# Sliding-window attention feeding a multiplicative FFN: batch 1's transposes moved into the weight fold, two products per unit in batch 1, the range check on Pool and a hinted branch

## Chip, cores, metric

One core of a Trainium2 chip runs the whole kernel. The metric is the device time of one execution in microseconds (us); a run's figure is the time of the slowest core, and here there is one.

## What is computed

Attention over a window of 64 keys (8 batches, 8 heads, 576 tokens, head size 64), then a feed-forward layer whose two branches are multiplied, on 4608 tokens of width 512:

```python
scores = scale * np.matmul(q, k.transpose(0, 1, 3, 2))
mask = (rel >= 0) & (rel < window)            # rel = query - key, window = 64
scores = np.where(mask, scores, -1000000000.0)
scores = scores - np.max(scores, axis=-1, keepdims=True)
attn = np.exp(scores)
attn = attn / (np.sum(attn, axis=-1, keepdims=True) + 1e-09)
x = np.matmul(attn, v)                        # heads side by side: [4608, 512]
a = x @ w1                                    # [512, 1024]
b = x @ w2
out = (a * b @ w3) @ w_out                    # w3 [1024, 1024], w_out [1024, 512]
```

## The kernel before

The code runs under a manual schedule: what is written first is issued first on its engine, so the order of the Python statements is the order of the work on PE, DVE, ACT, Pool and SP. Nothing is reordered by a scheduler.

**Attention.** A batch is six units, numbered `d` (batch 0 has 0 to 5, batch 1 has 6 to 11, batch 2 begins at 12). A unit is two pairs of heads on 192 queries. `scores(d)` (line 267) makes 4 matmuls into PSUM tile `s_ps`, an Exp on ACT (L282) into `pt`, and band masks by pairs of affine selects on Pool (L291, L293): four selects for the first two units of a batch, two for the others. `values(d)` (line 297) makes 8 matmuls (L312) into `o_ps` that carry the row sums beside the values, two Ln and one Exp on ACT (L321 to L324) and two multiplies on DVE (L327, L328) into `xT`. No maximum is subtracted; the logarithms of the sums are kept (`keep_sums`, L333, DMAs from SP's queue into `lnsum`), and at the end `check_sums` tests that they lie in bounds and counts those that don't. After all stores, `tc.If(bad > 0)` (L644) runs a general path if the count isn't zero.

**Transposes.** Q and K come as f32 (`load_qk`), are cast to f16 (`cast_qk` in two halves, L216; `cast_third` for batch 0, L223), and are transposed by PE in three groups of six blocks (`transposes`, L254). A group goes into PSUM tile `tp`, of which there is one, or into one half of a `spare` tile, made from the two banks of `s_ps` or `o_ps`. DVE evacuates K (L258); each Q group is evacuated by ACT for the one half of the partitions and DVE for the other (both L263).

**Fold.** At the start w3 and w_out are folded into one matrix `wc`, in 8 steps: `fold_t` transposes a piece of w3 (8 transposes L447, evacuated by DVE at L449 into `t2k`), `fold_mm` multiplies it (8 matmuls L455, cast into `wc_sb` at L456). One fold step stands behind each unit of batch 0.

**Products.** Each group of 512 tokens needs 8 `ffn_ab` (8 matmuls of 512 columns, L396; ACT copies `a` at L401, DVE multiplies by `b` at L402) and 4 `ffn_o` (8 matmuls L409; copy by DVE at L411, store by SP at L418). There are 9 groups, so 108 products of 8 matmuls. Group 0's are written out by hand among the units of batch 1. From batch 2 on a table `slots` gives each product a due unit, and `tick(u)` issues the attention up to it, with the transposes, casts and loads of later batches from the table `late`.

**Fillers.** `keep_busy(n)` (line 473) makes n small matmuls on the identity into `tp` that compute nothing needed. `ones_of(i)` (L489) writes the ones beside V, once for each of two V buffers, on Pool.

**End of the program.** After `tick` has issued the last attention unit, 12 products are left; `check_sums` is issued after the 4th of those counted by `quiet` (line 633), on DVE and one PE matmul (L470).

Of the kernel before, what the change touches and what calls it, by code (L numbers as in the profile page):

```python
# [15 lines left out]
P = 128  # L16
# [128 lines left out]
def kernel(  # L145
# [100 lines left out]
    def transposes(b, which, c, tp=None, late=True):  # L246

        if c == 0 and which == "k":
            kTs[b] = sb.tile([P, NJ, S], FP16, name="kT")
        t16 = (k16s if which == "k" else q16s)[b]  # L250
        if tp is None:
            tp = ps_t.tile([P, 6, P], FP16, name="tp")
        for i in range(6):
            nc.tensor.transpose(tp[:, i, :], t16[:, 6 * c + i, :], ident16)  # L254
        src = tp.rearrange("q i (p j) -> q j p i", p=TP)
        if which == "k":
            cp = dve_cp if late or c != 1 else act_cp
            cp(kTs[b].rearrange("q j (p i) -> q j p i", i=TI)[:, :, :, 6 * c:6 * c + 6], src)  # L258
        else:
            qT = qTs[b % 2]  # L260
            for lo, a, cp in ((0, 0, act_cp), (D, 1, dve_cp)):
                dst = qT[lo:lo + D, :, a, :].rearrange("q j (p i) -> q j p i", i=TI)
                cp(dst[:, :, :, 6 * c:6 * c + 6], src[lo:lo + D])  # L263
# [193 lines left out]

    def check_sums():

        rows = 2 * 3 * B  # L460
# [3 lines left out]
        okv = const.tile([rows, 1], FP32)  # L464
        nc.vector.tensor_reduce(okv, chk, axis=mybir.AxisListType.X, op=ALU.min)
        nc.vector.tensor_scalar(okv, okv, -1.0, 1.0, op0=ALU.mult, op1=ALU.add)
        ones = const.tile([rows, 1], FP32)
        nc.vector.memset(ones, 1.0)
        c_ps = ps_t.tile([1, 1], FP32, name="tp")
        nc.tensor.matmul(c_ps, okv, ones, start=True, stop=True)  # L470
        nc.vector.tensor_copy(bad_i[0:1, :], c_ps)
# [19 lines left out]
    ones_of(0)  # L491
    load_wo()
# [4 lines left out]
    ones_of(1)  # L497
# [9 lines left out]
    def spare(pool, name):  # L507

        t = pool.tile([P, 2, 512], FP32, name=name).bitcast(FP16)
        return [t[:, i, 0:768].rearrange("p (i n) -> p i n", i=6) for i in range(2)]  # L510
# [23 lines left out]
    for d in range(6):  # L534
# [6 lines left out]
        if d == 0:  # L541
            load_v(1, 0, 2)
        if d == 1:
            load_v(1, 3)
            load_qk(1, "k", nc.vector.memset)
            load_qk(1, "q")
# [16 lines left out]
    transposes(1, "k", 1)  # L563
    ffn_ab(0, 0)
    transposes(1, "k", 2)
    ffn_ab(0, 1)
    tps = spare(ps_v, "o_ps")
    for c in range(3):
        transposes(1, "q", c, tps[c] if c < 2 else None)
    ffn_ab(0, 2)  # L570
    load_v(1, 5)
    scores(6)
    copy_v(1, 1)
    ffn_ab(0, 3)
    scores(7)
    for d in range(6, 12):
        values(d)
        if d < 10:
            scores(d + 2)
            ffn_ab(0, d - 2)  # L580
        else:
            ffn_o(0, d - 10)
            store()
        if d == 7:
            copy_v(1, 4)
            load_qk(2, "k", nc.gpsimd.memset)
            load_qk(2, "q")
            load_v(2, 0, 2, 3)
        if d == 9:
            load_v(2, 4, 5)  # L590
    cast_qk(2, "k", 0, pool_cp)
    cast_qk(2, "k", 1, pool_cp)
    transposes(2, "k", 0)
    ffn_o(0, 2)
    store()
    transposes(2, "k", 1)
    ffn_o(0, 3)
    store()
    transposes(2, "k", 2)
    cast_qk(2, "q", 0, pool_cp)  # L600
    cast_qk(2, "q", 1, pool_cp)
    load_qk(3, "k")
# [7 lines left out]
    for g in range(1, NG):  # L610
# [8 lines left out]
    todo = {0: [lambda: transposes(2, "q", 0), lambda: copy_v(2, 1)],  # L619
            1: [lambda: transposes(2, "q", 1), lambda: copy_v(2, 4), lambda: cast_qk(3, "k", 0, pool_cp)],  # L620
            2: [lambda: transposes(2, "q", 2), lambda: cast_qk(3, "k", 1, pool_cp)]}
    u = 24
    quiet = 0
    for i, (w, due) in enumerate(slots):
        store()
        w()
        for fn in todo.get(i, []):
            fn()
# [10 lines left out]
    assert u == NU + LAG + 5 and quiet >= 4  # L639
# [4 lines left out]
    with tc.If(bad > 0, preferred_fallthrough_block=False):  # L644
# [30 lines left out]
```

## Time and profile before

| what | value |
|---|---|
| time, median of 3 runs | 317.93 us (316.24 to 318.02) |
| time of the profiled execution | 317.97 us |
| span of the profile (first to last instruction) | 316.2 us |
| PE busy | 280.5 us, 89% |
| DVE, ACT, POOL busy | 201.9, 176.8, 179.1 us |
| chain that ended last, by engine | PE 73%, DVE 9%, ACT 7%, issue 4%, POOL 4% |

The span begins at 0 with the first instruction. The profiled execution lasted 1.8 us longer than its span. The page gives busy time by engine and by group of instructions; a timeline lists instructions in order of their start, with the idle time of the engine just before them in brackets and the instruction that ended it; the view of stretches gives for each stretch the busy time of every engine and, as PEclk, the granted clock of PE (1.00 is full, 0.50 is half).

### The profile page before, as it was taken

What the parts mean: (1) busy time and instruction counts of PE and PEld (TensorE: products, weight loads), DVE (VectorE), ACT (ScalarE), POOL (GpSimd) and SP (SyncE); (2) the same over time, 40 slices, a digit from 0 to 9 for tenths busy, and PEclk for the clock granted to TensorE, in tenths of its full rate; (3) what the DMA queues carried; (4) which work ended last, traced back from release to release, by engine and by line L of the source; (5) the groups of instructions that cost most, each with busy time, mean ns of one, the idle gap of its engine ahead of it and who ended that gap; (6) DMA issues with size and microseconds to landing.
All of it is one profiled execution on the core that took longest, in us unless ns stands there. A gap on an engine that the chain in (4) does not pass through costs nothing.

```text
span 316.2 us, 5497 instructions
## 1 busy us (share of the span) xinstructions
PE 280.5 (89%) x2027; PEld 165.4 (52%) x2027; DVE 201.9 (64%) x307; ACT 176.8 (56%) x294; POOL 179.1 (57%) x211
## 2 busy tenths in 40 slices
PE   8578959677897999999999999999999999996880
PEld 8465524344354465655555797555555555542330
DVE  6646586645577478678777866598678655445340
ACT  2333723577334677786777665587588756522200
POOL 9664980079906896789669554885694452200000
PEclk9869997999999799999999999999999999999796
DMA  7999997006969294766729370940190030030021
GB/s 256 215 180 198 207 286 77 0 1 122 267 234 391 97 84 136 293 43 103 261 106 91 131 290 2 158 55 1 66 143 2 2 134 2 0 135 0 4 102 41
DMA packets 51668, 38.87 MB, mean 123 GB/s; under 512 B 38784, under 2 KB 41856, under 8 KB 51632
## 3 DMA queue, kind: packets, MB, share of 16 engines
q0 software_dynamic: 41744, 9.96, 34.5%
q1 hardware_dynamic: 9888, 28.46, 24.9%
q8 instruction: 18, 0.29, 0.4%
q14 instruction: 18, 0.15, 0.2%
HBM read 38.80 MB, written 9.44 MB: 153 GB/s over the span
## 4 chain that ended last, share of the span: by engine, by line
PE 73%; DVE 9%; ACT 7%; issue 4%; POOL 4%; DVEq 0%; POOLq 0%; ACTq 0%
PE f_ps L396 33%; PE f_ps L409 18%; PE o_ps L312 6%; PE s_ps L277 5%; PE tp L254 4%; PE tp L477 3%; DVE qT L263 2%; PE f_ps L455 2%; POOL pt L291 2%; ACT ln_s L322 2%; ACT qT L263 2%; ACT r L324 2%; DVE xT L328 1%; POOL pt L293 1%; ACT pt L282 1%
## 5 line engine op out<-in xcount | busy, mean ns | idle before, releaser
L396 PE MATMUL f_ps<-xT,w_sb 128*128 128x512 f16 (+1 forms) x640 | 137.5, 364 | 0.7 <-DVE ab L402 0.7
L291 POOL TENSOR_SCALAR_AFFINE_SELECT pt<-pt 128x512 f16<-128x512 f16 (+1 forms) x64 | 52.8, 825 | 74.6 <-ACT pt L282 74.6
L396 PEld LDWEIGHTS <-w_sb 128*128 128x128 f16 x640 | 60.9, 99 | 52.2 <-issue 4.6
L409 PE MATMUL f_ps<-wc_sb,ab 128*128 128x512 f16 x288 | 67.1, 379 | 0.1
L402 DVE TENSOR_TENSOR ab<-f_ps,a_sb 128x512 f16<-128x512 f32 x72 | 49.7, 691 | 24.1 <-PE f_ps L396 20.1
L401 ACT COPY a_sb<-f_ps 128x512 f32<-128x512 f32 x72 | 41.7, 579 | 33.3 <-PE f_ps L396 32.7
L282 ACT ACTIVATE pt<-s_ps 128x1024 f16<-128x1024 f32 (+1 forms) x48 | 45.6, 950 | 24.9 <-PE s_ps L277 22.4
L327 DVE TENSOR_TENSOR xT<-o_ps,r 64x384 f16<-64x384 f32 x48 | 26.4, 549 | 48.3 <-ACT r L324 45.9
L293 POOL TENSOR_SCALAR_AFFINE_SELECT pt<-pt 128x512 f16<-128x512 f16 (+1 forms) x64 | 52.8, 825 | 4.4
L321 ACT ACTIVATE ln_s<-o_ps 64x384 f32<-64x384 f32 x48 | 23.4, 487 | 45.8 <-PE o_ps L312 45.8
L409 PEld LDWEIGHTS <-ab 128*128 128x128 f16 x288 | 27.0, 98 | 27.6 <-issue 0.3
L235 POOL DMA_DIRECT2D v<-in_v_dram x40 | 34.7, 873 | 4.7 <-DMA ab<-in_moe_w_out_dram 2.9
L312 PE MATMUL o_ps<-pt,v 128*128 128x128 f16 (+1 forms) x384 | 28.0, 215 | 8.2 <-DVE xT L328 4.3
L312 PEld LDWEIGHTS <-v 128*128 128x128 f16 x384 | 23.6, 98 | 20.8 <-issue 6.6
L411 DVE COPY t2k<-f_ps 128x512 f32<-128x512 f32 x36 | 24.9, 692 | 9.5 <-PE f_ps L409 8.8
L277 PE MATMUL s_ps<-qT,kT 128*128 128x256 f16 x192 | 27.9, 269 | 1.5 <-DVE qT L263 0.9
L328 DVE TENSOR_TENSOR xT<-o_ps,r 64x384 f16<-64x384 f32 x48 | 26.9, 561 | 0.6
L324 ACT ACTIVATE r<-ln_s 128x384 f32<-128x384 f32 x48 | 25.1, 523 | 1.5
L277 PEld LDWEIGHTS <-kT 128*128 128x128 f16 x192 | 18.1, 100 | 11.4 <-issue 2.7
L263 DVE COPY qT<-tp 64x768 f16<-64x768 f16 x20 | 19.2, 960 | 7.6 <-ACT qT L263 7.3
L322 ACT ACTIVATE ln_s<-o_ps 64x384 f32<-64x384 f32 x48 | 23.1, 482 | 0.6
L258 DVE COPY kT<-tp 128x768 f16<-128x768 f16 x21 | 20.0, 951 | 1.8 <-PE tp L254 1.6
(61 smaller groups left out, 200.2 us busy)
## 6 DMA issues: line engine op xcount, KB each, us to landing
stage<-in_k_dram SPq DMA_DIRECT2D x16, 576.0 KB
stage<-in_q_dram SPq DMA_DIRECT2D x16, 576.0 KB
out_dram<-t2k SPq DMA_DIRECT2D x36, 256.0 KB
v<-in_v_dram POOLq DMA_DIRECT2D x32, 128.0 KB, 5.1
w_sb<-in_moe_w_dram POOLq DMA_DIRECT2D x4, 512.0 KB, 9.1
ab<-in_moe_w_out_dram POOLq DMA_DIRECT2D x1, 1024.0 KB, 11.9
ab<-in_moe_w_dram POOLq DMA_DIRECT2D x2, 512.0 KB, 14.3
xT<-in_moe_w_dram POOLq DMA_DIRECT2D x2, 512.0 KB, 18.1
```

The lines of the kernel that those rows point to most:

```text
L235: nc.gpsimd.dma_start(out=vh[lo:P, c], in_=v[b, :, s0:s0 + P - lo, :].rearrange("h s d -> s h d"))
L263: cp(dst[:, :, :, 6 * c:6 * c + 6], src[lo:lo + D])
L277: nc.tensor.matmul(s_ps[:, jj, c0:c0 + 2 * n].rearrange("k (a n) -> k a n", a=2), kT[:, 2 * jp + jj, k0:k0 + P], qT[:, 2 * jp + jj, :, q0: ...
L282: nc.scalar.activation(pt[:, :, 0:w], s_ps[:, :, 0:w], AF.Exp, bias=-SHIFT, scale=scale)
L291: nc.gpsimd.affine_select(out=sl, in_=sl, pattern=pat, compare_op=ALU.is_ge, fill=0.0, base=off, channel_multiplier=-1)
L293: nc.gpsimd.affine_select(out=sl, in_=sl, pattern=[[-s, m] for s, m in pat], compare_op=ALU.is_ge, fill=0.0, base=63 - off, channel_multip ...
L312: nc.tensor.matmul(o_ps[:, jj, o0:o0 + n], v16[:, si * 2 + bi, j0 + jj, a * D:a * D + P], pt[:, jj, c0 + a * n:c0 + a * n + n], start=firs ...
L324: nc.scalar.activation(r, y, AF.Exp, scale=-1.0)
L396: nc.tensor.matmul(d[:, f * n + c0:f * n + c1], w[:, dc, (fc + f) * P:(fc + f + 1) * P], xT[:, dc, xc:xc + c1 - c0], start=first, stop=(dc ...
L401: act_cp(a_sb[:, 0:nf * n], a_ps[:, 0:nf * n])
L402: nc.vector.tensor_tensor(ab[:, fc:fc + nf, lo:hi], b_ps[:, 0:nf * n].rearrange("p (f n) -> p f n", f=nf), a_sb[:, 0:nf * n].rearrange("p ...
L409: nc.tensor.matmul(o_ps, ab[:, fc, t * P:t * P + P], wc_sb[:, fc, :], start=(fc == 0), stop=(fc == 7))
```

## The change

**Start.** The second `ones_of` is issued ahead of the weight loads on Pool instead of behind them. The evacuation of batch 0's three Q groups is written so that ACT and DVE take turns on the tiles (q0 on ACT with q1 on DVE, q2 on ACT with q0 on DVE, q1 on ACT with q2 on DVE), where before ACT and DVE took the same tile one after the other. `keep_busy` before `scores(0)` has 15 matmuls for 10, and there is one more of 10 before the fold. `transposes` returns the evacuating function if asked (`evac=False`), and `spare` makes its tile as f16 `[P, 2, 1024]`.

**End of the fold.** Batch 1's K casts stand behind unit 3, one unit earlier. Its K and Q transposes stand around unit 5 and the last fold step, all through `s_ps` spares and `tp`; before, they were spread over the first three products of group 0.

**Batch 1.** Units 6 to 9 have two products each, 10 one, and none stands between `scores(7)` and `values(6)`. Batch 2's Q and K are loaded at the end of the fold, and cast by Pool at units 7 to 10. Its transposes stand around unit 11 with three products left beside them; before, seven products stood between them, and the Q groups ran beside group 1's first three (table `todo`, which is gone).

**First units of batch 2.** The due times of group 1 rise by a quarter of the lead with each of its first four products (`ahead`); before, the first three were due at once.

**Check and branch.** The square and the comparison move from DVE to Pool and are issued after the 2nd of the last products; the count (`count_bad`: one PE matmul and a cast on DVE) after the 6th. The If is laid out with its true block as the fall-through, so that the compare itself jumps past the general path; a branch hint is named at the place of the count.

The diff, cut to its core:

```diff
@@ transposes @@
-            for lo, a, cp in ((0, 0, act_cp), (D, 1, dve_cp)):
-                dst = qT[lo:lo + D, :, a, :].rearrange("q j (p i) -> q j p i", i=TI)
-                cp(dst[:, :, :, 6 * c:6 * c + 6], src[lo:lo + D])
+        def half(a, cp):
+            dst = qT[a * D:a * D + D, :, a, :].rearrange("q j (p i) -> q j p i", i=TI)
+            cp(dst[:, :, :, 6 * c:6 * c + 6], src[a * D:a * D + D])
+        if not evac:
+            return half
+        half(0, act_cp)
+        half(1, dve_cp)
@@ check_sums @@
-        nc.vector.tensor_tensor(chk, lnsum, lnsum, ALU.mult)
-        nc.vector.tensor_single_scalar(chk, chk, BOUND * BOUND, op=ALU.is_le)
+        nc.gpsimd.memset(ones, 1.0)
+        nc.gpsimd.tensor_tensor(chk, lnsum, lnsum, ALU.mult)
+        nc.gpsimd.tensor_single_scalar(chk, chk, BOUND * BOUND, op=ALU.is_le)
         nc.vector.tensor_reduce(okv, chk, axis=mybir.AxisListType.X, op=ALU.min)
         nc.vector.tensor_scalar(okv, okv, -1.0, 1.0, op0=ALU.mult, op1=ALU.add)
-        nc.vector.memset(ones, 1.0)
+    def count_bad():
@@ start @@
     ones_of(0)
+    ones_of(1)
     load_wo()
...
-    ones_of(1)
     load_v(0, 4, 5)
...
-    transposes(0, "q", 0, tps[3])
-    transposes(0, "q", 1)
-    transposes(0, "q", 2, spare(ps_s, "s_ps")[0])
-    keep_busy(10)
+    q0 = transposes(0, "q", 0, tps[3], evac=False)
+    q1 = transposes(0, "q", 1, evac=False)
+    q2 = transposes(0, "q", 2, spare(ps_s, "s_ps")[0], evac=False)
+    q0(0, act_cp)
+    q1(1, dve_cp)
+    q2(0, act_cp)
+    q0(1, dve_cp)
+    q1(0, act_cp)
+    q2(1, dve_cp)
+    keep_busy(15)
     scores(0)
     keep_busy(10)
     scores(1)
+    keep_busy(10)
@@ fold @@
-    for d in range(6):
+    for d in range(5):
...
         if d == 0:
             load_v(1, 0, 2)
+            load_qk(1, "k", nc.vector.memset)
+            load_qk(1, "q")
...
         if d == 3:
             load_v(1, 4)
-        if d == 4:
             cast_qk(1, "k", 0, dve_cp)
             cast_qk(1, "k", 1, dve_cp)
-            cast_qk(1, "q", 0, pool_cp)
-            transposes(1, "k", 0)
+    cast_qk(1, "q", 0, pool_cp)
     cast_qk(1, "q", 1, dve_cp)
+    tps = spare(ps_s, "s_ps")
+    transposes(1, "k", 0, tps[0])
+    transposes(1, "k", 1, tps[1])
+    values(5)
+    transposes(1, "k", 2)
+    fold_step(7)
...
+    tps = spare(ps_s, "s_ps")
+    transposes(1, "q", 0, tps[0])
+    transposes(1, "q", 1, tps[1])
+    transposes(1, "q", 2)
@@ batch 1 @@
+    steps = [lambda fc=fc: ffn_ab(0, fc) for fc in range(2, 8)] + [lambda t=t: ffn_o(0, t) for t in range(3)]
+    for d in range(6, 11):
         values(d)
         if d < 10:
             scores(d + 2)
-            ffn_ab(0, d - 2)
+        for _ in range(2 if d < 10 else 1):
+            steps.pop(0)()
+            store()
...
+    tps = spare(ps_s, "s_ps")
+    transposes(2, "k", 0, tps[0])
+    transposes(2, "k", 1, tps[1])
+    values(11)
+    transposes(2, "k", 2)
...
     ffn_o(0, 3)
...
+    transposes(2, "q", 0, tps[0])
+    transposes(2, "q", 1, tps[1])
+    transposes(2, "q", 2)
@@ slots @@
-        first = 3 if g == 1 else 0
-            share = max(0, i + 1 - first) / (len(part) - first)
-            slots.append((w, lo + (hi - lo) * share + (LAG + 1) * (i >= first)))
+            ahead = (LAG + 1) * (min(1, (i + 1) / 4) if g == 1 else 1)
+            slots.append((w, lo + (hi - lo) * (i + 1) / len(part) + ahead))
@@ end @@
-            if quiet == 4:
+            if quiet == 2:
                 check_sums()
+            if quiet == 6:
+                count_bad()
+                tc.mark_branch_hint_location("range", "LikelyTaken", mybir.ALL_ENGINES)
...
-    with tc.If(bad > 0, preferred_fallthrough_block=False):
+    with tc.If(bad > 0, preferred_fallthrough_block=True, label="range"):
```

In the changed kernel the lines stand 4 to 20 further down: the select pairs are L297 and L299, values L318, products L402 and L415, their evacuations L408 and L417, the fold L453 to L462, the If L664.

Three places show how the order moves. The first is Pool at the start, where `v_0_85` and `v_1_86` are the two V buffers with their ones, and the DMAs behind them fetch w_out, pieces of w3 and blocks of V. Before:

```order
L489 MEMSET v_0_85 128x48x64
L434 DMA ab<-in_moe_w_out_dram 128x8x512
L440 DMA ab<-in_moe_w_dram 128x2x1024
L235 DMA v_0_85<-in_v_dram 128x8x64 x3
L440 DMA ab<-in_moe_w_dram 128x2x1024
L440 DMA xT<-in_moe_w_dram 128x2x1024 x2
L489 MEMSET v_1_86 128x48x64
```

Of the change:

```order
L498 MEMSET v_0_85 128x48x64
L498 MEMSET v_1_86 128x48x64
L440 DMA ab<-in_moe_w_out_dram 128x8x512
L446 DMA ab<-in_moe_w_dram 128x2x1024
L235 DMA v_0_85<-in_v_dram 128x8x64 x3
L446 DMA ab<-in_moe_w_dram 128x2x1024
L446 DMA xT<-in_moe_w_dram 128x2x1024 x2
```

The second memset now stands ahead of all weight loads.

The second place is DVE at the end of the fold, from the cast of `wc` of fold step 5 to the last evacuation of batch 1's Q. Before:

```order
L456 CAST wc_sb<-f_ps 128x512
L216 CAST k_597<-stage 128x18x64 x2
L258 COPY kT<-tp 128x128x6
L327 TENSOR_TENSOR xT<-o_ps,r 64x2x192
L328 TENSOR_TENSOR xT<-o_ps,r 64x2x192
L216 CAST q_600<-stage 128x18x64
L258 COPY kT<-tp 128x128x6
L402 TENSOR_TENSOR ab<-f_ps,a_sb 128x512
L258 COPY kT<-tp 128x128x6
L402 TENSOR_TENSOR ab<-f_ps,a_sb 128x512
L263 COPY qT_88<-o_ps 64x4x32x6 x2
L263 COPY qT_88<-tp 64x4x32x6
```

Of the change:

```order
L216 CAST k_578<-stage 128x18x64 x2
L333 TENSOR_TENSOR xT<-o_ps,r 64x2x192
L334 TENSOR_TENSOR xT<-o_ps,r 64x2x192
L455 COPY t2k<-f_ps 128x1024
L462 CAST wc_sb<-f_ps 128x512
L216 CAST q_618<-stage 128x18x64
L258 COPY kT<-s_ps 128x128x6 x2
L333 TENSOR_TENSOR xT<-o_ps,r 64x2x192
L334 TENSOR_TENSOR xT<-o_ps,r 64x2x192
L258 COPY kT<-tp 128x128x6
L264 COPY qT_88<-s_ps 64x4x32x6 x2
L264 COPY qT_88<-tp 64x4x32x6
```

The products' multiplies (L402) no longer stand between the evacuations, and the K casts stand one fold step earlier. The first group of a spare tile is evacuated before the second group's transposes into the other half are let go, in both kernels.

The third place is DVE at the check. Before, behind the fifth product from the last attention unit:

```order
L402 TENSOR_TENSOR ab<-f_ps,a_sb 128x512 x5
L462 TENSOR_TENSOR chk<-lnsum 48x768
L463 TENSOR_SCALAR chk<-chk 48x768
L465 TENSOR_REDUCE okv<-chk 48x1
L466 TENSOR_SCALAR okv<-okv 48x1
L468 MEMSET ones 48x1
L471 CAST bad_i<-tp 1x1
L402 TENSOR_TENSOR ab<-f_ps,a_sb 128x512 x3
```

Of the change:

```order
L408 TENSOR_TENSOR ab<-f_ps,a_sb 128x512 x3
L474 TENSOR_REDUCE okv<-chk 48x1
L475 TENSOR_SCALAR okv<-okv 48x1
L408 TENSOR_TENSOR ab<-f_ps,a_sb 128x512 x4
L480 CAST bad_i<-tp 1x1
L408 TENSOR_TENSOR ab<-f_ps,a_sb 128x512
L417 COPY t2k<-f_ps 128x512 x4
```

The reduce stands two products earlier, and four products stand between it and the cast of the count. On every engine's list a row BRANCH_PREFETCH_HINT stands at the very start of the program, behind the first jump, and the unconditional jump behind the compare is gone.

More of the change, by code (lines that the diff above doesn't have):

```diff
@@ L244, with transposes @@
     kTs = {}
-    def transposes(b, which, c, tp=None, late=True):
+    def transposes(b, which, c, tp=None, late=True, evac=True):
         if c == 0 and which == "k":
@@ L507, in spare @@
     def spare(pool, name):
[L509 removed]
+        t = pool.tile([P, 2, 1024], FP16, name=name)
         return [t[:, i, 0:768].rearrange("p (i n) -> p i n", i=6) for i in range(2)]
@@ L579 @@
             scores(d + 2)
-            ffn_ab(0, d - 2)
-        else:
[L582 to L596, printed above, removed]
+        for _ in range(2 if d < 10 else 1):
+            steps.pop(0)()
+            store()
+        if d == 6:
+            load_v(2, 4, 5)
+            copy_v(1, 4)
+            load_qk(3, "k")
+        else:
+            which, hh = [("k", 0), ("k", 1), ("q", 0), ("q", 1)][d - 7]
+            cast_qk(2, which, hh, pool_cp)
+    tps = spare(ps_s, "s_ps")
[3 more added lines that the diff above has]
+    transposes(2, "k", 2)
+    for hh in range(2):
+        cast_qk(3, "k", hh, pool_cp)
     ffn_o(0, 3)
     store()
[L599 to L602, printed above, removed]
+    tps = spare(ps_s, "s_ps")
+    transposes(2, "q", 0, tps[0])
+    transposes(2, "q", 1, tps[1])
+    transposes(2, "q", 2)
+    copy_v(2, 1)
+    copy_v(2, 4)
     load_qk(3, "q")
@@ L638 @@
     store()
-    assert u == NU + LAG + 5 and quiet >= 4
+    assert u == NU + LAG + 5 and quiet >= 6
     fast.close()
```

34 lines of the change are left out of this document (11 added, 23 removed).

## Prediction

> **What bounds the kernel now.** I read the page's sums first, then the view of stretches, cut where the program's stages meet: start, fold to unit 2, end of the fold with batch 1's transposes, batch 1 with batch 2's transposes, first units of batch 2, steady state.
>
> ```profile
> span 316.2 us, 5497 instructions
> ...
> 0.00:20.50 20.50, 14.07 (x149) 13.35 (x150) 12.53 (x13) 6.67 (x8) 14.72 (x19) 0.84 1.19 219
> 20.50:37.30 16.80, 14.74 (x127) 8.86 (x126) 9.40 (x18) 8.61 (x14) 12.07 (x17) 0.99 1.31 184
> 37.30:61.20 23.90, 17.37 (x128) 9.58 (x129) 16.79 (x25) 9.93 (x17) 9.17 (x10) 0.93 0.74 153
> 61.20:98.50 37.30, 31.27 (x213) 16.54 (x213) 22.85 (x38) 21.48 (x36) 24.04 (x28) 1.00 0.77 171
> 98.50:110.50 12.00, 10.23 (x71) 5.63 (x71) 6.03 (x8) 6.81 (x12) 9.01 (x13) 0.86 0.51 202
> 110.50:281.20 170.70, 169.92 (x1247) 101.77 (x1246) 122.67 (x189) 118.59 (x200) 110.05 (x127) 1.00 0.51 100
> ```
>
> After the bounds and the length come PE, PEld, DVE, ACT and POOL busy, then the granted clock. From 110.5 on PE works 169.92 of 170.70 us: nothing but less PE work would help there, and the change takes none away. Idle PE lies ahead of that (6.4 us at the start, 2.1, 6.5, 6.0, 1.8) and behind it. A product costs 8 x 0.216 = 1.73 us at full clock (row L396 of the check's fence: 24 matmuls at full clock would be 5.2). The change can save only idle time and half-clock time in these stages.
>
> The clock follows idleness. These stretches are 3.3 to 3.5 us long:
>
> ```profile
> 44.60:48.10 3.50, 0.87 (x15) 0.87 (x16) 2.87 (x5) 0.00 (x0) 2.02 (x2) 0.99 1.26 207
> 48.10:51.50 3.40, 3.40 (x12) 1.16 (x10) 2.30 (x4) 1.49 (x3) 0.00 (x0) 0.50 1.37 137
> 55.00:58.30 3.30, 1.41 (x17) 0.94 (x16) 1.98 (x3) 1.29 (x2) 0.00 (x0) 1.00 0.00 0
> 99.30:102.70 3.40, 1.63 (x20) 1.19 (x19) 1.91 (x2) 1.40 (x2) 2.60 (x5) 1.00 1.02 412
> 102.70:106.10 3.40, 3.40 (x10) 1.31 (x9) 1.15 (x3) 2.08 (x4) 3.27 (x5) 0.50 0.58 236
> ```
>
> PE 0.87 busy of 3.50 was followed by 3.4 us at half clock, and so was 1.63 of 3.40; 1.41 of 3.30 was not. A half-clock stretch costs 1.7 us where PE is the bound.
>
> **Check (E).** The first of the two holes behind 281.2:
>
> ```profile
> 282.54 0.48 SPq L333 DMA_DIRECT2D lnsum<-ln_s  x1
> ...
> 286.65 0.69 DVE L402 TENSOR_TENSOR ab<-f_ps,a_sb 128x512 f16<-128x512 f32 x1 [1.04 <-PE f_ps L396]
> ...
> 293.46 0.19 PE L470 MATMUL tp<-ones,okv 48*1 48x1 f32 x2 [3.46 <-DVE ones L468]
> 293.58 7.04 PE L396 MATMUL f_ps<-xT,w_sb 128*128 128x512 f16 x24
> ```
>
> PE stood 3.46 us for the count's matmul, and then 24 product matmuls took 7.04 us, 1.8 more than at full clock. With four products between the reduce and the count, both go, and the count's own 0.1 stays: 3.46 + 1.84 - 0.1 = **-5.2**. The cover: the last sums are issued at 282.54, and the DMA view of 282 to 286 us, in slices of 0.1, ends with this traffic:
>
> ```profile
> GB/s 410 348 103 0 0 0 0 0 0 143 348 369 471 369 389 328 267 0 0 0 0 0 82 0 0 0 0 0 0 0 0 0 0 0 0 0 0 0 0 0
> ```
>
> The last of it lies in the 23rd slice, so they have landed by 284.3. The reduce stands on DVE behind the third product's multiply, done at 286.65 + 0.69 = 287.3. So Pool has 3.0 us for two operations of 768 columns (the memset of 48 x 1 beside them waits for nothing) that this trace does not have on Pool. Nearest rows:
>
> ```profile
> L291 POOL TENSOR_SCALAR_AFFINE_SELECT pt<-pt 128x1024 f16<-128x1024 f16 x32 | 36.0, 1124 | 38.3 <-ACT pt L282 38.3
> ...
> L489 POOL MEMSET v<- 128x3072 f16 x2 | 5.4, 2684 | 0.0
> ```
>
> At 0.87 to 1.10 ns a column, 768 take 0.7 to 0.85 us each, 1.7 for both. Two f32 inputs may cost several times that; at 3 us each the reduce, and with it DVE's next product multiply, would come 2.9 us late, so the gain's bounds are -5.4 and -2.3. I take -5.2, since the rows lie near.
>
> **Branch (F).** From the lists by source line, with durations in ns (min/median/max) and first and last start:
>
> ```profile
> L644 PEldq COMPARE_BRANCH  x2: 95/1872/3650, 304.2 to 307.7; - x2
> L644 DVEq COMPARE_BRANCH  x2: 51/53/55, 308.2 to 308.4; - x2
> L644 SPq COMPARE_BRANCH  x2: 38/46/53, 309.3 to 311.8; - x2
> ```
>
> ```profile
> L670 SPq EVENT_SEMAPHORE  x14: 17/28/28, 314.6 to 316.2; - x14
> ...
> L670 DVEq DRAIN  x2: 10/34/59, 311.8 to 315.7; - x2
> ```
>
> SP compares at 309.3, falls through, waits for the stores until 311.8, jumps past the general path, and shows its next instruction at 314.6: 2.75 us for a jump. DVE's took 3.4. After the change the compare at 309.3 is the jump, beside the landing of the stores. Without help from the hint SP arrives at 309.3 + 2.75 to 3.4 = 312.05 to 312.7 instead of 314.6, so -2.55 to -1.9; with the target fetched ahead the stores set the end, -2.8. If a second jump stays behind the first, its 3.4 eats all this and 0.7 more. I take **-2.2**, without help: the hint is issued 300 us ahead of the branch.
>
> **Start (A).**
>
> ```profile
> L223 DVE CAST k<-stage x2: 560/741/922, 6.6 to 7.0; 128x768 f16<-128x768 f32 x2
> L223 DVE CAST q<-stage x2: 541/1300/2060, 11.6 to 13.6; 128x768 f16<-128x768 f32 x2
> ```
>
> ```profile
> 13.72 0.67 PE L254 MATMUL o_ps<-ident,q 128*128 128x128 f16 x6 [2.47 <-DVE q L223]
> ...
> 15.26 0.96 DVE L263 COPY qT<-o_ps 64x768 f16<-64x768 f16 x1 [1.13 <-ACT qT L263]
> ...
> 17.15 1.23 PE L477 MATMUL tp<-ident 128*128 128x128 f16 x10 [1.48 <-DVE qT L263]
> ...
> 20.52 1.18 PE L447 MATMUL f_ps<-ident,ab 128*128 128x128 f16 x16
> ```
>
> DVE's first q cast took 2.06 us where others take 0.55, beside Pool's 2.7 us memset. With the memset earlier the cast ends 1.5 sooner. DVE's evacuations now start on q1 while ACT has q0, instead of 1.13 late, three of 0.96 in a row: from about 13.0 to 16.0, where before the third ended at 17.01 + 0.96 = 17.97. That is -2.0, and ten more fillers ahead of the fold give back 0.7 to 1.2: **-1.3**. Pool's memset now delays the issue of the weights by 2.7 us. I estimate that this costs nothing, since K and Q hold the DMA engines for the first 8 us anyway; at worst all 2.74 arrive at the fold, which then starts 0.9 late. Bounds -1.7 and +0.9.
>
> **End of the fold (B).** Before, 37.3 to 61.2 us, with three products in it. Its DVE rows, and the wait in its middle:
>
> ```profile
> 41.25 0.68 DVE L456 CAST wc_sb<-f_ps 128x512 f16<-128x512 f32 x1
> ...
> 45.37 1.80 DVE L216 CAST k<-stage 128x1152 f16<-128x1152 f32 x2
> 47.23 0.51 PE L254 MATMUL tp<-ident,k 128*128 128x128 f16 x6 [3.77 <-DVE k L216]
> ...
> 47.78 0.96 DVE L258 COPY kT<-tp 128x768 f16<-128x768 f16 x1 [0.60 <-PE tp L254]
> ...
> 49.79 0.55 DVE L327 TENSOR_TENSOR xT<-o_ps,r 64x384 f16<-64x384 f32 x1 [1.06 <-ACT r L324]
> ```
>
> After the change DVE is a chain from fold step 5's cast on, which ends 4.65 us into the stage: K casts 1.80 (6.45), two multiplies 1.15 (7.6), w3 copy and wc cast 1.4 (9.0), Q cast 0.76 (9.75), first kT 0.96 (10.7). Only then may the second K group use the tile's other half (0.5), and values(5) stands behind it on PE (0.6), its Ln, Ln, Exp take 1.6 (13.35), multiplies 1.15 (14.5), third kT 0.96, first Q half 0.96 (16.4), second Q group 0.5, ACT's half 0.81, DVE's two 1.92: 19.7. One product is inside; the other two cost 3.46 later: 19.7 + 3.5 - 23.9 = -0.7. To that I add 1.2: PE waits from about 6.95 to 10.7 as it did for 3.77 before, so the clock falls again, this time with the transposes and values(5) on the chain. And 0.4, since the K casts fall beside Pool's selects, as the two took 1.80 beside a Pool DMA issue instead of 1.5; 0 to 1.2. Together **+0.9** (-1.5 to +2).
>
> [...]
>
> **Batch 1 (C).**
>
> ```profile
> 71.63 0.61 PE L312 MATMUL o_ps<-pt,v 128*128 128x128 f16 x8 [0.71 <-DVE xT L328]
> ...
> 75.11 0.61 PE L312 MATMUL o_ps<-pt,v 128*128 128x128 f16 x8 [0.71 <-DVE xT L328]
> ```
>
> A unit takes 3.48 us, of which PE waits 0.71 for the multiplies of the unit before. With two products a unit PE has 0.44 + 0.45 + 2 x 1.73 = 4.4 and waits for nothing. So 3.7 to values(6), as now, four units of 4.4, then the same serial chain as in B without casts: multiplies end 3.15 after values(10) starts, t2k 0.69 and kT 0.96 (4.8), second K group and values(11) 0.95, Ln to multiplies 2.65 (8.4), kT 0.96, t2k 0.69, Q 0.96 (11.0), group 0.4, ACT 0.81, DVE 1.92: 14.1. Sum 35.4 with 12 products, before 37.3 with 13: -0.2. Two gaps of PE of about 2.5 and 3 us are new there, with one product between them; by the stretch 99.3 to 102.7 the clock falls: +0.9, since half of what runs then waits anyway. **+0.7** (-1.5 to +2.5).
>
> [...]
>
> **First units of batch 2 (D).**
>
> ```profile
> 99.94 0.49 PE L277 MATMUL s_ps<-qT,kT 128*128 128x256 f16 x4 [0.62 <-ACT pt L282]
> ...
> 102.22 0.45 PE L312 MATMUL o_ps<-pt,v 128*128 128x64 f16 x7 [0.65 <-POOL pt L293]
> ...
> 108.42 0.50 PE L312 MATMUL o_ps<-pt,v 128*128 128x128 f16 x8
> ```
>
> From scores(12), at 98.5, to values(13), at 108.42, 9.9 us hold two products, waits on Exp and selects, and 1.7 of half clock. After the change a product stands between the two scores and another ahead of values(12): three products, three scores, one values and three transposes are 5.2 + 1.35 + 0.45 + 1.2 = 8.2 without a wait. 8.2 - 1.73 - 9.9 = **-3.5** (-4 to -1, if the clock falls here anyway).
>
> **Sum.** -1.3 + 0.9 + 0.7 - 3.5 - 5.2 - 2.2 = -10.6, to the profiled execution's 317.97 (the span 316.2 and 1.8 around it; the median of the runs shown is 317.93): **307.4 us**.
>
> **The rivals.** (1) The clock holds in the transposes' gaps and casts and selects miss each other: B and C lose their 1.2, 0.4 and 0.9, 304.9 us. For it: 55.0 to 58.3. Against: the other two stretches. (2) The front end nets nothing: the serial chains behind half tiles give back what A and D bring; E and F alone make 310.6. For it: the chain's many evacuations, each of which adds its semaphore hops, and DVE has 16.8 of 23.9 us busy in B already. Against: D's waits are plainly gone. (3) The check or the branch brings little: Pool slow, 310.3, or no gain from the jump, 309.6. For it: no Pool arithmetic on two f32 inputs in the trace; against: 3.0 us of cover. (4) Slower: the hint, at the program's start, turns each engine's instruction fetch away from its sequential path, and later fetches are not ahead of the engine. The place is PE, the price that of its 3.65 us behind the branch for each lost fetch; the third makes up the gain, from the fourth it is slower, five give 307.4 + 18.3 = 325.7. For it: only that price; against: nothing says that a hint acts before its branch. (5) Rivals (2) and (3) together: a check that keeps only its 2.3 and nothing else, 315.7. That the change doesn't do what it says: a hint too early is that for the branch, and is already left out of F.
>
> **Numbers.** Forecast 0.37, (1) 0.2, (2) 0.18, (3) 0.13, (4) 0.05, (5) 0.07. A measurement of this kernel tells about 1%, 3.2 us, from no change. All of the first four are faster by more: 0.88. (5) is within 1%: 0.07. (4) is 0.05. The range takes in (1) with a prefetched branch and some of C below, and (2) with part of (3) above: 303 to 313.
>
> **What would show it.** Right: no PE idle over 0.3 us behind the last attention unit and full clock there; SP's next instruction 2.7 to 3.4 us behind its compare at the end, with no wait between; the fold's first transposes at about 19.2; units of 4.4 us in batch 1 with no wait; no wait and full clock from scores(12) to values(13). Wrong: DVE waiting for Pool's square by 2 us or more; half clock for 6 us or more between the end of the fold and batch 2; weight landings that hold up the fold.

## The result

The changed kernel took 308.81 us (median of 4 executions, 305.97 to 310.44), the kernel before 317.98 beside it (4 executions): ratio 0.9705, 95% interval 0.9619 to 0.9791. With more executions (the change again, below) it is 0.9700, 0.9654 to 0.9746. That is a gain of 9.1 to 9.6 us (by medians and by ratios), where 10.6 were forecast. The profiled execution is the longest of the four, 310.44 us with a span of 308.6, 7.6 less than before.

The stretches of the changed kernel, cut at the same events as those of before (the columns are PE, PEld, DVE, ACT and POOL busy, then the clock):

```profile
0.00:19.60 19.60, 12.50 (x164) 11.74 (x164) 11.10 (x13) 7.48 (x9) 13.35 (x17) 1.00 1.06 216
19.60:37.50 17.90, 16.14 (x124) 9.41 (x125) 9.48 (x18) 7.80 (x13) 13.52 (x18) 0.90 1.32 231
37.50:60.60 23.10, 16.35 (x112) 9.43 (x113) 16.59 (x24) 8.77 (x15) 12.40 (x14) 0.79 1.65 253
60.60:97.20 36.60, 30.74 (x206) 16.81 (x205) 20.82 (x32) 20.78 (x35) 21.16 (x24) 0.95 0.31 87
97.20:109.30 12.10, 11.72 (x94) 7.00 (x94) 9.20 (x15) 8.83 (x15) 10.30 (x15) 1.00 0.57 219
...
281.60:302.80 21.20, 21.16 (x99) 9.28 (x97) 9.38 (x15) 4.69 (x8) 3.60 (x2) 1.00 0.16 56
302.80:308.60 5.80, 0.00 (x0) 0.00 (x0) 0.69 (x1) 0.00 (x0) 0.00 (x0) 0.84 0.23 82
```

Read it by the marks of the program. The first scores of batch 2 start at 97.19 instead of 98.49, with three products fewer done; values(13) at 105.35 instead of 108.42, with two fewer. Two products are 3.46 us, so up to there this execution is 0.4 us behind the kernel before, not 3.2 ahead. PE then works almost without a break to 302.8 at full clock. What the profiled execution gained lies behind 281.6.

By the terms of the prediction, in this execution, and for the front also in four more. Four of the runs below leave the change's front as it is (the change again, the old check, the check on DVE, no hint), and the last column is from their profiles, against the same profile of the kernel before. E is PE's time from the first of the last products' matmuls (281.20 before, 281.58 here) to its last matmul, F the rest of the span.

| term | forecast | measured | from | four more profiles |
|---|---|---|---|---|
| A, start, at unit 3 | -1.3 | +0.2 | 37.27 to 37.50 | -1.6 to -0.4 |
| B, end of the fold | +0.9 | +2.7 | 23.93 to 23.14, two products fewer in it | +1.0 to +2.5 |
| C, batch 1 | +0.7 | +1.0 | 37.29 to 36.55, one product fewer | +0.8 |
| D, first units of batch 2 | -3.5 | -3.5 | 9.93 to 8.16, one product more | -3.5 |
| E, check | -5.2 | -5.2 | 26.33 to 21.18 | |
| F, branch | -2.2 | -2.8 | 8.67 to 5.84 | |

The profiled execution is the worst of the five for the front: the other four stand 0.7 to 2.2 us ahead of the kernel before at values(13). None reaches the 3.2 of the forecast.

**Start.** The second row is PE's first fold step in the timeline, with its wait in brackets.

```profile
11.29 1.05 DVE L223 CAST q<-stage 128x768 f16<-128x768 f32 x2
...
19.63 1.57 PE L453 MATMUL f_ps<-ident,ab 128*128 128x128 f16 x16 [1.65 <-DMA ab<-in_moe_w_dram]
...
21.14 4.74 PE L461 MATMUL f_ps<-ab,t2k 128*128 128x512 f16 x16
```

The casts are short, as forecast, 1.05 us for two. But PE was ready for the fold at 17.98 and waited 1.65 us for w3, whose load Pool had issued 2.8 us later than before; then the clock fell, and 16 matmuls took 4.74 us instead of 3.63. The 0.9 us at the fold's start were gone by the next transposes of w3 (25.71 against 25.49 before). In the other four profiles of this front the fold starts at 18.76 to 19.99, after waits for w3 of 0.17 to 1.41 us, and the 16 matmuls take 3.63: the clock lost there is of this execution, the wait is of all.

**End of the fold.** From the timeline, DVE and PE:

```profile
42.19 2.48 DVE L216 CAST k<-stage 128x1152 f16<-128x1152 f32 x2
...
48.74 0.80 PE L254 MATMUL s_ps<-ident,k 128*128 128x128 f16 x6 [3.50 <-DVE kT L258]
49.33 1.06 PE L318 MATMUL o_ps<-pt,v 128*128 128x128 f16 x8
...
50.82 3.54 PE L461 MATMUL f_ps<-ab,t2k 128*128 128x512 f16 x8
...
56.73 0.50 PE L254 MATMUL s_ps<-ident,q 128*128 128x128 f16 x6 [2.03 <-DVE qT L264]
...
57.40 3.45 PE L402 MATMUL f_ps<-xT,w_sb 128*128 128x512 f16 x8
```

The chain runs as worked out up to the second K group, whose wait for the first one's evacuation is 3.50 us. Then three half-clock windows (stretches of 3.41 us each) follow where one was counted: the last fold product takes 3.54 us (1.73 at full clock) with the Q groups queued behind it, and the first product takes 3.45 with scores(6) behind it. Three of the other four profiles of this front lose three windows here as well, the one without the hint loses one.

**Check.**

```profile
281.58 12.32 PE L402 MATMUL f_ps<-xT,w_sb 128*128 128x512 f16 x56
...
284.76 1.46 POOL L472 TENSOR_TENSOR chk<-lnsum 48x768 f32<-48x768 f32 x1 [12.68 <-DMA lnsum<-ln_s]
...
286.32 2.14 POOL L473 TENSOR_SCALAR chk<-chk 48x768 f32<-48x768 f32 x1
...
288.49 0.94 DVE L474 TENSOR_REDUCE okv<-chk 48x1 f32<-48x768 f32 x1 [0.77 <-POOL chk L473]
...
293.84 0.19 PE L479 MATMUL tp<-ones,okv 48*1 48x1 f32 x2
```

Pool took 1.46 and 2.14 us, about twice the 1.7 taken for both, and DVE's reduce waited 0.77 for it. PE did not wait: the count's matmul has no idle time ahead of it and the 56 product matmuls before it ran in one row.

**Branch.** The If's line by engine, and then SP's first instructions behind it:

```profile
L664 SPq EVENT_SEMAPHORE  x8: 17/17/17, 305.0 to 306.9; - x8
...
L664 PEldq COMPARE_BRANCH  x1: 398/398/398, 299.4 to 299.4; - x1
...
L664 SPq COMPARE_BRANCH  x1: 70/70/70, 304.5 to 304.5; - x1
```

```profile
L690 SPq EVENT_SEMAPHORE  x14: 17/28/28, 307.0 to 308.5; - x14
```

SP compares at 304.5 and is past the general path at 305.0; then it waits for the stores until 306.9. PE's jump takes 0.4 us where it took 3.65.

### The profile page after: what moved, and what is told of

Read it like the earlier page. It is cut to its first block, busy times and chain, and to the rows that moved or that the text cites. A ratio compares the mean times of both kernels' runs of the same rounds, so it can differ in the third digit from the quotient of the medians.

```text
span 308.6 us, 5529 instructions
## 1 busy us (share of the span) xinstructions
PE 280.1 (91%) x2042; PEld 165.8 (54%) x2042; DVE 199.9 (65%) x304; ACT 176.3 (57%) x294; POOL 183.1 (59%) x214
## 4 chain that ended last, share of the span: by engine, by line
PE 76%; DVE 7%; POOL 5%; ACT 4%; DMA 4%; issue 2%; POOLq 0%; DVEq 0%; ACTq 0%
PE f_ps L402 37%; PE f_ps L415 20%; PE o_ps L318 6%; PE s_ps L283 5%; DMA ab<-in_moe_w_dram 4%; PE tp L254 3%; PE f_ps L461 3%; POOL v L498 2%; DVE xT L334 1%; ACT r L330 1%; ACT ln_s L328 1%; POOL pt L299 1%; POOL pt L297 1%; PE s_ps L254 1%; DVE qT L264 1%
## 5 line engine op out<-in xcount | busy, mean ns | idle before, releaser
L402 PE MATMUL f_ps<-xT,w_sb 128*128 128x512 f16 (+1 forms) x640 | 135.7, 361 | 0.7 <-DVE ab L408 0.7
L297 POOL TENSOR_SCALAR_AFFINE_SELECT pt<-pt 128x512 f16<-128x512 f16 (+1 forms) x64 | 52.7, 824 | 78.7 <-ACT pt L288 78.7
L402 PEld LDWEIGHTS <-w_sb 128*128 128x128 f16 x640 | 60.7, 98 | 52.3 <-issue 3.4
L415 PE MATMUL f_ps<-wc_sb,ab 128*128 128x512 f16 x288 | 68.3, 386 | 0.1
L408 DVE TENSOR_TENSOR ab<-f_ps,a_sb 128x512 f16<-128x512 f32 x72 | 49.8, 691 | 19.4 <-PE f_ps L402 16.5
L299 POOL TENSOR_SCALAR_AFFINE_SELECT pt<-pt 128x512 f16<-128x512 f16 (+1 forms) x64 | 53.0, 828 | 4.4
L415 PEld LDWEIGHTS <-ab 128*128 128x128 f16 x288 | 27.4, 99 | 29.0 <-issue 1.9
L318 PEld LDWEIGHTS <-v 128*128 128x128 f16 x384 | 24.1, 99 | 14.8 <-ACT pt L288 2.3
L318 PE MATMUL o_ps<-pt,v 128*128 128x128 f16 (+1 forms) x384 | 28.3, 217 | 3.2 <-POOL pt L299 1.3
L417 DVE COPY t2k<-f_ps 128x512 f32<-128x512 f32 x36 | 24.8, 692 | 9.2 <-PE f_ps L415 8.5
L264 DVE COPY qT<-tp 64x768 f16<-64x768 f16 x18 | 17.3, 960 | 8.8 <-ACT qT L264 8.2
L461 PE MATMUL f_ps<-ab,t2k 128*128 128x512 f16 x64 | 17.7, 430 | 0.0
```

Of the source, the lines that this page charges most:

```text
L297: nc.gpsimd.affine_select(out=sl, in_=sl, pattern=pat, compare_op=ALU.is_ge, fill=0.0, base=off, channel_multiplier=-1)
L299: nc.gpsimd.affine_select(out=sl, in_=sl, pattern=[[-s, m] for s, m in pat], compare_op=ALU.is_ge, fill=0.0, base=63 - off, channel_multip ...
L318: nc.tensor.matmul(o_ps[:, jj, o0:o0 + n], v16[:, si * 2 + bi, j0 + jj, a * D:a * D + P], pt[:, jj, c0 + a * n:c0 + a * n + n], start=firs ...
L402: nc.tensor.matmul(d[:, f * n + c0:f * n + c1], w[:, dc, (fc + f) * P:(fc + f + 1) * P], xT[:, dc, xc:xc + c1 - c0], start=first, stop=(dc ...
L408: nc.vector.tensor_tensor(ab[:, fc:fc + nf, lo:hi], b_ps[:, 0:nf * n].rearrange("p (f n) -> p f n", f=nf), a_sb[:, 0:nf * n].rearrange("p ...
L415: nc.tensor.matmul(o_ps, ab[:, fc, t * P:t * P + P], wc_sb[:, fc, :], start=(fc == 0), stop=(fc == 7))
```

## The experiments

Each ran in 5 or 6 executions beside 11 of the kernel before on the same chip. A ratio is to the kernel before, with its 95% interval; differences in us are worked out from ratios times 318.5, and those to the change are against its 0.9700, whose interval is itself 1.5 us to either side. A difference to the change of less than about 1.8 us is therefore not clear of noise.

### The old front with the new end

The kernel before, with the change's `check_sums`, `count_bad`, hint and If:

```diff
-            if quiet == 4:
+            if quiet == 2:
                 check_sums()
+            if quiet == 6:
+                count_bad()
+                tc.mark_branch_hint_location("range", "LikelyTaken", mybir.ALL_ENGINES)
...
-    with tc.If(bad > 0, preferred_fallthrough_block=False):
+    with tc.If(bad > 0, preferred_fallthrough_block=True, label="range"):
```

> The kernel before up to the last products, with the check on Pool, the late count and the hinted branch of the change. Theory: the check and the branch carry the gain and the front of the program nets between +0.4 (the profiled execution) and -1.2 (the median), so 310 us, 8 below the kernel before and 0 to 1.5 above the change. Rival, the prediction's own sum: the front brings 3.2, so 312 us or more. Rival two: the front costs time in every execution, so below 308.

Measured 310.12 us, 0.9727 (0.9701 to 0.9754): 8.7 us below the kernel before. Check and branch carry almost all of the gain. And the change itself once more, to set beside it:

> The change itself with more rounds, to set its front beside the run with the old front (ratio 0.9727 to the kernel before). Theory: the front nets between +0.4 and -1.2 us, ratio 0.969 to 0.974. Rival, the prediction's sum of start, transposes and first units (-3.2): ratio 0.9627 or less.

309.20 us, 0.9700 (0.9654 to 0.9746). The front nets 0.9 us, between a loss of 1 and a gain of 2.5 by the intervals. The prediction's 3.2 (ratio 0.9627) lies outside.

### The check

First everything back on DVE behind the fifth product:

```diff
-        nc.gpsimd.memset(ones, 1.0)
+        nc.vector.memset(ones, 1.0)
...
-        nc.gpsimd.tensor_tensor(chk, lnsum, lnsum, ALU.mult)
-        nc.gpsimd.tensor_single_scalar(chk, chk, BOUND * BOUND, op=ALU.is_le)
+        nc.vector.tensor_tensor(chk, lnsum, lnsum, ALU.mult)
+        nc.vector.tensor_single_scalar(chk, chk, BOUND * BOUND, op=ALU.is_le)
...
-            if quiet == 2:
+            if quiet == 4:
                 check_sums()
-            if quiet == 6:
                 count_bad()
```

> The change with square, comparison, reduce and count together on DVE behind the fifth of the last products, as before. Theory: the hole of 3.4 us and half-clock products come back whole, +5.1 to +5.3, 314 us. Rival: the half clock in that place was chance of the executions profiled, and only +3.4 comes back, 312 us.

314.43 us, 0.9867 (0.9832 to 0.9902): 5.3 us above the change. Its profile has both parts of the hole again, the wait of 3.4 us and the product matmuls at half clock, which speaks against the rival:

```profile
291.48 0.18 PE L479 MATMUL tp<-ones,okv 48*1 48x1 f32 x2 [3.47 <-DVE okv L475]
291.60 7.99 PE L402 MATMUL f_ps<-xT,w_sb 128*128 128x512 f16 x24
```

Then only the first half of that edit, DVE in place of Pool, with the new places kept:

> The change with the square and the comparison back on DVE, but issued behind the third product and the count still four products later. Theory: the distance between reduce and count is what removes the hole, and Pool adds little: no PE idle over 0.3 us behind the last attention unit, within 0.7 us of the change, 309 us. Rival: DVE blocked for 2.6 us keeps the products' PSUM tiles, PE waits 1 us or more in the third or fourth product, 310 to 311 us.

308.03 us, 0.9659 (0.9625 to 0.9694), no slower than with Pool. Its timeline:

```profile
285.80 0.69 DVE L408 TENSOR_TENSOR ab<-f_ps,a_sb 128x512 f16<-128x512 f32 x1 [1.03 <-PE f_ps L402]
286.42 0.95 DVE L472 TENSOR_TENSOR chk<-lnsum 48x768 f32<-48x768 f32 x1
...
287.99 0.94 DVE L474 TENSOR_REDUCE okv<-chk 48x1 f32<-48x768 f32 x1
...
289.04 1.29 DVE L408 TENSOR_TENSOR ab<-f_ps,a_sb 128x512 f16<-128x512 f32 x2
```

DVE is taken for 2.6 us, makes up the product's multiply behind it, and PE's 56 product matmuls from 280.35 on take 12.25 us without a break up to the count's. What removed the hole is the distance between reduce and count, not Pool.

### The hint

```diff
-                tc.mark_branch_hint_location("range", "LikelyTaken", mybir.ALL_ENGINES)
```

> The change without the branch hint, with the If laid out as in the change. Theory: the hint is what makes the taken jump short (0.4 to 0.7 us on every engine in the trace of the change against 2.6 to 3.4 before), so the jumps take 2.6 to 3.4 us again and SP's next instruction stands 0.2 to 1.0 us later against the landing of the stores: +0.2 to +1.0, 309 to 310 us. Rival: the layout alone makes the jump short, no difference in the jump's length in the trace.

309.54 us, 0.9712 (0.9684 to 0.9739), too near to the change to tell by time. The trace tells it:

```profile
L663 SPq EVENT_SEMAPHORE  x8: 17/17/17, 304.6 to 305.2; - x8
...
L663 PEldq COMPARE_BRANCH  x1: 3962/3962/3962, 296.8 to 296.8; - x1
...
L663 SPq COMPARE_BRANCH  x1: 50/50/50, 301.9 to 301.9; - x1
```

SP compares at 301.9 and goes on at 304.6, 2.7 us; PE's compare takes 3.96. With the hint it was 0.5 and 0.4. From SP's compare to the end of the span are 5.0 us here and 4.1 in the change's profile, so the hint brings 0.9 there; the kernel before took 6.9, and the 1.9 left are put down to the layout, by subtraction. In the twelve profiles with the hint this stretch lasted 3.2 to 4.2 us, and SP waited for the stores in it. The prediction had taken the hint to do nothing, since it runs 300 us ahead.

### The start

The memset in its old place, everything else as in the change:

```diff
     ones_of(0)
-    ones_of(1)
     load_wo()
...
         load_w3(n)
+    ones_of(1)
     load_v(0, 4, 5)
```

> The change with the second memset back in its old place behind the weight loads, the evacuations still taken in turn. Theory: Q casts 1.5 us late again, but weights 1.2 early; the two cancel, fold at 19.3 to 20, within 0.8 of the change. Rival, as the prediction had it: the casts decide, +1.5 to +2, 310.5 us or more.

310.67 us, 0.9750 (0.9720 to 0.9781), 1.6 us above the change. This is the rival's number, though by time alone not clear of noise. The trace bears it out: the casts were late again (2.80 us for two) and the fold started at 21.72, where the nine profiles with the early memset have 18.76 to 19.99. The clock fell for two windows, but it did so in two of those nine as well (fold at 19.80 and 19.99), so it is not the casts alone. Next, weights first and the memset still out of the casts' way:

```diff
     ones_of(0)
-    ones_of(1)
     load_wo()
...
-    load_v(0, 4, 5)
...
+    gate = const.tile([P, 1], FP16)
+    pool_cp(gate, q16s[0][:, TI - 1, P - 1:P])
+    ones_of(1)
+    load_v(0, 4, 5)
```

> The change with the weight loads issued first on Pool again and the second memset behind batch 0's third Q cast (a copy of one column from that cast's result holds Pool until then). Theory: in the change the early memset frees DVE's casts but moves the w3 landing from 18.35 to 19.6 us, and PE waits 1.65 us for it; here both come early, the fold starts at about 18.4 instead of 19.6, and the time is 1.2 shorter, or up to 2.9 where this also keeps PE's clock at the fold: 306 to 308 us. Rival: the landing is set by the DMA queues and not by the issue on Pool, fold at 19.6, no difference.

307.23 us, 0.9656 (0.9617 to 0.9694), 1.4 below the change, inside the noise, and 3.0 below the late memset, which is clear of it.

```profile
18.61 1.07 PE L453 MATMUL f_ps<-ident,ab 128*128 128x128 f16 x16 [1.13 <-DMA ab<-in_moe_w_dram]
```

The fold starts at 18.61 and at full clock. The last run below, with the same start, has 18.38; both lie ahead of all nine profiles with the early memset, in each of which PE waited for w3 (0.17 to 2.10 us). So the landing does follow the issue on Pool, by about 1 of its 2.7 us. The prediction had estimated that it costs nothing.

### The waits of PE in the transposes

Fillers in the waits, with nothing else moved:

```diff
     transposes(1, "k", 0, tps[0])
+    keep_busy(45)
     transposes(1, "k", 1, tps[1])
...
     transposes(1, "q", 0, tps[0])
+    keep_busy(25)
```

and the same with 30 and 25 for batch 2.

> The change with filler matmuls on the identity (45, 25, 30 and 25) between the first and the second group of batch 1's and batch 2's K and Q transposes, where PE waits 2 to 3.5 us. They take only time that PE waits anyway. Theory: the half-clock stretches 47.4 to 54.2, 57.5 to 60.9 and 88.1 to 91.5 come from those waits, and their share on the chain is 2 to 3.5 us: 305.5 to 307 us, with full clock from the end of the fold to batch 2. Rival: the waits set the chain and the clock costs nothing beside them, within 0.7 of the change.

305.90 us, 0.9596 (0.9568 to 0.9625), 3.3 below the change, and the five executions lie within 0.8 us of each other (the change's six above within 3.5). The clock stays full from 23 us to the end of PE's work. So about 3 us of what the transposes cost were clock and not waiting. Three views of stretches show it for stage B alone, from unit 3 to scores(6): the change again, no hint, and the fillers.

```profile
36.72:59.67 22.95, 16.19 (x112) 9.55 (x113) 16.60 (x24) 8.77 (x15) 12.42 (x14) 0.78 1.64 260
36.70:58.21 21.51, 14.04 (x113) 8.83 (x113) 16.05 (x23) 8.66 (x15) 12.43 (x14) 0.92 1.71 250
37.19:57.81 20.62, 16.33 (x183) 11.59 (x184) 16.05 (x23) 8.66 (x15) 12.42 (x14) 1.00 1.78 241
```

The stage lasts 22.95 us with three half-clock windows, 21.51 with one and 20.62 with none. Then the waits themselves, taken away by other tiles:

```diff
     transposes(1, "k", 0, tps[0])
-    transposes(1, "k", 1, tps[1])
+    transposes(1, "k", 1)
     values(5)
-    transposes(1, "k", 2)
+    transposes(1, "k", 2, tps[1])
...
-    tps = spare(ps_s, "s_ps")
-    transposes(1, "q", 0, tps[0])
-    transposes(1, "q", 1, tps[1])
-    transposes(1, "q", 2)
+    qa = transposes(1, "q", 0, evac=False)
+    qb = transposes(1, "q", 1, spare(ps_s, "s_ps")[0], evac=False)
+    qc = transposes(1, "q", 2, spare(ps_v, "o_ps")[0], evac=False)
+    qa(0, act_cp)
+    qb(1, dve_cp)
+    qc(0, act_cp)
+    qa(1, dve_cp)
+    qb(0, act_cp)
+    qc(1, dve_cp)
```

and the same for batch 2.

> The change with batch 1's and batch 2's second K group in tile tp and the third in the spare's other half, and with the three Q groups in three tiles (tp, s_ps, o_ps) evacuated by ACT and DVE in turn as at the start. Theory: the second group's wait for the first's evacuation, with values(5) and values(11) queued behind it on PE, is what makes the serial chains long; values(5) starts 3 to 4 us earlier and scores(6) and scores(12) 2 to 3 us earlier each: 303 to 305 us. Rival: DVE's own work (casts, multiplies, copies) sets the chain's length, so less than 1.5 us in all.

300.54 us, 0.9436 (0.9406 to 0.9467), 8.4 below the change. PE's rows at the end of the fold:

```profile
43.48 0.51 PE L254 MATMUL s_ps<-ident,k 128*128 128x128 f16 x6 [1.05 <-DVE k L216]
...
43.83 0.50 PE L254 MATMUL tp<-ident,k 128*128 128x128 f16 x6
...
44.61 0.61 PE L318 MATMUL o_ps<-pt,v 128*128 128x128 f16 x8 [0.28 <-DVE xT L334]
...
53.68 0.50 PE L283 MATMUL s_ps<-qT,kT 128*128 128x256 f16 x4 [0.74 <-DVE qT L264]
```

The second group follows the first at once; values(5) is 4.7 us earlier than in the change's profile, scores(6) 7.0 and scores(12) 10.9 us, of which 1.25 were there at unit 3 already; the change's profile is of its longest execution. The clock is full here too to the end of PE's work, so the 8.4 can hold the 3.3 of the fillers. One of its six executions took 1015.27 us and is outside the ratio; no profile of it exists, so whether the check counted a sum and the general path ran, or something else did, is open. The last run below, with the same edit in it, didn't show it in six executions; neither is to be used before it is explained.

The two halves of that edit by themselves, K first:

> The change with only the K half of the run before (second K group in tp, third in the spare's other half), batch 1 and batch 2. Theory: values(5) and values(11), which wait on PE behind the second group in the change, start 3 us earlier, and by the rows of the change this is worth 2.4 us a batch (0.9 of DVE's wait for the second group and 1.5 for the Ln and Exp behind values): 304 us, 4 to 6 below the change. Rival: the chain behind it (Q groups) takes all of it up again, under 1.5.

305.68 us, 0.9581 (0.9542 to 0.9621), 3.8 below the change.

> The change with only the Q half (three tiles, ACT and DVE in turn). Theory: the second Q group's wait of 1.9 to 2.0 us and 0.6 of ACT ahead of DVE in each batch go: 2.3 a batch, 304.5 us; with the K half of the run beside it the two sum to the 8 of both. Rival: either half alone leaves PE idle enough for the clock to fall as in the change, so each brings under 2 and only both together bring the 8.

304.68 us, 0.9552 (0.9515 to 0.9588), 4.7 below. They sum to 8.5 against the 8.4 of both, as waits do that are in series on one chain with neither hidden behind the other. How much of each is clock is not told apart: in stages B and C the profile of the K half loses three half-clock windows, that of the Q half one, that of both none. At last both halves, the gated memset and the check on DVE:

> The change with both halves, the memset behind the Q casts with the weights first on Pool, and the square and comparison on DVE behind the third product. Theory: the fold starts 0.7 to 1.2 us earlier than with both halves alone, and the check is the same on DVE as on Pool: 299 to 300 us. Rival: what the start gains is lost in the wait for the next pieces of w3, 300.5 us.

300.04 us, 0.9417 (0.9385 to 0.9450), 9.0 below the change and 18.6 below the kernel before. The fold starts at 18.38. Against both halves alone that is 0.6 us, inside the intervals: whether the start's gain adds up here is not told. Six executions lay between 298.38 and 300.61.

## Why the prediction was right and where it was not

**Right, with its reason.** E was read as the idle time ahead of the count plus the half-clock products behind it, 5.2; the profile gives 5.2 and undoing it 5.3. Distance between the reduce and the count was to remove both, and it does so with DVE in Pool's place as well. D was read as waits that a product between the scores would fill, 3.5; all five profiles give 3.5. C came out at +0.8 to +1.0 for +0.7, with units of 4.3 to 4.5 us where 4.4 were forecast.

**Right in sum, wrong in a price.** Pool's two operations were priced at 0.7 to 0.85 us and took 1.46 and 2.14. DVE's reduce came 0.77 us late by it, which the prediction would have charged to the gain, but no product waited. F was priced without the hint, at 2.2; the hint works, SP goes on 0.5 us behind its compare where 2.7 to 3.4 were to show, and the stores' landing sets the end, the -2.8 that stood as a bound.

**Wrong: the front.** The sum took -3.2 for A to D; the runs give -0.9, and the profiled execution +0.4. That is nearer to rival (2), a front that nets nothing, which had 0.18, than to the forecast, which had 0.37. Two of the three signs named for being wrong appeared: 13.7 us at half clock between the end of the fold and batch 2, and weight landings that hold up the fold.

The step that failed most is the 1.2 for the clock in B. The chain itself was right: forecast at 19.7 us and 0.4 for the casts, it took 20.62 at full clock with the fillers, and its waits are in the trace where they were put. But PE's waits brought three half-clock windows in four of five profiles, not one, and two products on whose end the transposes or the scores waited ran in them. That cost 2.0 to 2.5 us; the one profile with a single window has B at +1.0, the forecast's +0.9. The fillers give the price of the clock alone, 3.3 us over B and C, against the 2.1 in the sum. In A, "I estimate that this costs nothing" for the weights issued 2.7 us later failed as well: PE waited 0.2 to 2.1 us for them. How much of A's shortfall that makes is not settled, since the gated memset's 1.4 us are inside the noise.

That the total came out within 1.1 us is in part luck: the front brought 2.3 us less than its terms and the end 1.3 more (8.7 us in the run with the old front, for 7.4 in E and F), and the two errors offset each other.

**Casts in B, gaps in C.** The K casts beside Pool's selects took 2.48 us where 2.2 was in the sum, so 0.3 more came in B, and Pool's select took 1.53 instead of 1.12 beside them. In C, PE's gaps were 2.31 and 1.89 us where about 2.5 and 3 were forecast, and the clock fell behind the first: the product between them took 3.47 us where others take 1.89.

## To carry to other kernels

In this kernel a half of a PSUM tile whose other half is still being read was no second buffer (PE waited 3.50 us for it): before ordering work around a wait, look at which tile the wait is for, since other tiles brought as much here as check and branch together, 8.4 us against 8.7 (with one execution left unexplained). The PE waits in the transposes cost clock beside their length, 3.3 us by the fillers: price a PE wait also by the products that run at half clock behind it. This check was taken off the path by distance between producing and using its result, on either engine (5.3 us).

## What was not expected of the hardware

All half-clock stretches in both profiles start and end on one grid of 3.41 us, with different phases: the first edges lie at 2.96 and 0.25 us of the span. Two views of stretches on that grid, first the change, then the kernel before; the clock is the third number from the end:

```profile
16.62:20.03 3.41, 1.44 (x21) 1.25 (x21) 0.00 (x0) 1.07 (x2) 0.86 (x2) 1.00 1.96 172
20.03:23.44 3.41, 3.41 (x19) 1.79 (x16) 1.38 (x2) 0.00 (x0) 3.27 (x6) 0.50 1.39 186
43.92:47.34 3.42, 0.51 (x6) 0.39 (x7) 3.34 (x6) 0.00 (x0) 3.42 (x6) 1.00 1.28 202
47.34:50.75 3.41, 2.01 (x20) 2.01 (x20) 2.30 (x3) 0.33 (x1) 2.71 (x3) 0.50 1.92 170
50.75:54.16 3.41, 3.41 (x11) 1.25 (x10) 2.07 (x3) 1.17 (x3) 0.00 (x0) 0.50 2.94 114
54.16:57.58 3.42, 1.39 (x20) 1.14 (x19) 0.96 (x1) 1.60 (x3) 0.00 (x0) 1.00 0.99 365
57.58:60.99 3.41, 3.41 (x11) 1.35 (x10) 2.45 (x5) 1.77 (x3) 0.00 (x0) 0.50 1.01 414
...
91.71:95.12 3.41, 1.52 (x21) 1.17 (x19) 1.59 (x2) 1.46 (x2) 0.00 (x0) 1.00 0.46 117
```

```profile
54.86:58.27 3.41, 1.52 (x16) 0.99 (x15) 2.12 (x3) 1.39 (x2) 0.00 (x0) 1.00 0.00 0
58.27:61.69 3.42, 2.72 (x23) 1.53 (x20) 2.34 (x3) 1.98 (x3) 0.00 (x0) 1.00 0.00 0
99.23:102.65 3.42, 1.65 (x21) 1.19 (x19) 1.91 (x2) 1.47 (x2) 2.54 (x5) 1.00 1.02 410
102.65:106.06 3.41, 3.41 (x11) 1.27 (x9) 1.11 (x3) 2.08 (x4) 3.31 (x5) 0.50 0.59 241
```

In these two profiles a full-clock window with PE 1.44 us busy or less was always followed by a window at half clock. 1.52 was not, in both kernels, and 1.65 was. In the run with other tiles even 1.37 was not:

```profile
45.45:48.86 3.41, 1.37 (x11) 0.82 (x11) 3.37 (x6) 1.29 (x3) 3.36 (x5) 1.00 1.33 199
48.86:52.27 3.41, 3.08 (x28) 1.93 (x27) 2.79 (x4) 2.31 (x4) 0.00 (x0) 1.00 1.84 204
```

So busy time alone does not tell when the clock falls. A window at half clock with 2.01 busy was followed by another. The same front lost three windows in stage B in four profiles and one in the fifth, and none to two at the start; the clock of the change was 0.963 to 0.986 over four executions, and its time spread by 4.5 us. That the phase of the grid decides how many, by how a wait falls on the windows, is an estimate from the two phases above and not shown.

The branch hint at 0.8 us, the program's start, shortened the jump at its end, some 300 us later, from 2.7 to 0.5 us on SP, and PE's from 3.96 to 0.40.
